# Chunked delta-rule attention with a gated MLP on one core: all five engines ordered by a planner while the kernel is built, state matmuls woven as 64x64 tiles

## The chip, the cores and the metric

The kernel runs on one core of a Trainium2 chip. The metric is the device time of one execution in microseconds (us). Before the change it is 653.14 us, the median of three runs (652.49 to 659.39).

The engines are TensorE (PE; PEld is its weight load), VectorE (DVE), ScalarE (ACT), GpSimd (POOL) and SyncE (SP), whose queue issues the DMAs. Each runs its own list of instructions in a fixed order and waits on semaphores.

## The reference

An attention with a state matrix per head, updated token by token (4 batches, 8 heads, 768 tokens, head size 48), feeds a gated MLP that also mixes over the sequence:

```python
k_n = k / (np.linalg.norm(k, axis=-1, keepdims=True) + 1e-06)
for t in range(S):
    kt, vt, bt = (k_n[:, :, t], v[:, :, t], beta[:, :, t, None])
    y[:, :, t] = np.einsum('bhd,bhde->bhe', q[:, :, t], state)
    v_old = np.einsum('bhde,bhd->bhe', state, kt)
    state = state + bt[:, :, :, None] * np.einsum('bhd,bhe->bhde', kt, vt - v_old)
...
h = np.maximum(x @ w_in, 0.0)                       # 384 -> 1024, halves u and v
v_n = (v - mu) / np.sqrt(var + 1e-06)
v_s = np.einsum('ts,bsd->btd', w_spatial, v_n) + b_spatial[None, :, None]
return ((u * v_s) @ w_out).astype(np.float32)       # 512 -> 384
```

## The kernel before

**Steps.** A batch's 768 tokens are cut into 12 chunks of 64, so there are 48 steps of one chunk of one batch, all 8 heads (4 pairs `u` of two heads `h`). Batches 0 and 2 form one chain, 1 and 3 the other; the first 6 steps belong to the first chain alone, the last 6 to the second, between them the chains take turns (`ORDER`). Within a chain a step needs the state of the one before.

**Groups and lanes.** Four steps make a group `g`. For a group the kernel computes key norms (`group_norm`), the products of keys with keys and with queries (`products`, L360, TensorE), masks them with factors that GpSimd makes (`mask_c`, L342), and inverts unit triangular matrices. The inversion is the "lanes": the matrices go through DRAM (`ad`) into a layout with one matrix per lane, then `lanes` runs 30 pairs of a product (L550) and a subtraction (L557) on VectorE on a matrix `w` in one PSUM bank (`pw`), and the result goes through DRAM (`wd`) back into `ta`. The lanes invert 32x32 blocks; `step_e` (L595) and `step_f` (L607) complete each step's 64x64 matrix. Group 0 uses blocks of 16 (`lanes16`, L444 to L496).

**A step's state work**, each eight small fp32 matmuls: `step_a` (L652, subtracts what the state predicts from v; v was scaled by GpSimd, L638), `step_b` (L669, result scaled into `su` in two halves, L673), `step_c` (L688, new state, two halves, L692), `step_d` (L702, output, with 112 and 128 rows), `step_k` (L660, copies of the masked q-k product). Every fp32 matmul leaves two records in the trace.

**The MLP** takes 256 tokens at a time. `mlp_v` (L769), `mlp_u` (L830), `mlp_g` (L849, the mixing over the sequence, possible once a batch is complete) and `mlp_o` (L894) use 128x128 matmuls in three parts (high x high, high x low, low x high). Their after-work is in `post_v`, `post_g`, `post_o` (store L905). The weights `w_in` and `w_out` are 64-bit floats decoded on VectorE (`load_w`, L157, L203).

**Order.** The author's slots (`slot_a`, `slot_cd`, `slot_b`) write out each step; `fill` puts a budget of MLP matmuls between the slots, `lane` some lane operations. Only the preparation's VectorE work is bound by hand to the written order; elsewhere a list scheduler places instructions by priority:

```python
    with tc.manual_schedule(engines={ET.DVE}):
...
    with tile.TileContext(nc, schedule_with_timeline_sim=True) as tc:
```

PSUM is shared out as 3 banks `pa` (state), 2 `pq` (products), 2 `pm` (MLP) and 1 `pw` (lanes).

Of the kernel before, what the change touches and what calls it, by code (L numbers as in the profile page):

```python
# [19 lines left out]
G = 4  # L20
DM, DFF = 384, 1024
# [7 lines left out]
R0 = 1.5  # L29
TD = 1  # L30
TP = 4
G16 = 1
C16 = 1
W16 = 16
X1 = 14
R1 = 1.7
CAP = 3.0
NL = 4
LD = 3
XD = 3  # L40
HP = 300
NW = 3
EJ = 6
PD = 2
M3 = 99
M4 = 12
CI = 1
CQ = 0
LS = 2
LP = 0  # L50
CAP0 = 4.0
PE0 = 18
PG0 = 99
PG1 = 99
VN = 1
VL = 1
DEC = 1
M5 = 10
DQ = 2
LAG = 6  # L60
# [10 lines left out]
VB = 8  # L71
UB = 4
KQB=2
NPA=3
NPQ=2
# [3 lines left out]
def delta_rule_gated_mlp(  # L79
# [3 lines left out]
    kp_t: bass.AP,  # L83
    qb_t: bass.AP,
    qa_t: bass.AP,
    kv_nat: bass.AP,
    b_nat: bass.AP,
# [7 lines left out]
    PSUM = bass.MemoryType.PSUM  # L95
    const = ctx.enter_context(tc.tile_pool(name="const", bufs=1))
    grp = ctx.enter_context(tc.tile_pool(name="grp", bufs=2))
    live = ctx.enter_context(tc.tile_pool(name="live", bufs=3))
    work = ctx.enter_context(tc.tile_pool(name="work", bufs=2))
    moe = ctx.enter_context(tc.tile_pool(name="moe", bufs=2))  # L100
    dram = ctx.enter_context(tc.tile_pool(name="dram", bufs=2, space=bass.MemoryType.DRAM))
    pa = ctx.enter_context(tc.tile_pool(name="pa", bufs=NPA, space=PSUM))
    pq = ctx.enter_context(tc.tile_pool(name="pq", bufs=NPQ, space=PSUM))
    pm = ctx.enter_context(tc.tile_pool(name="pm", bufs=7 - NPA - NPQ, space=PSUM))
    pw = ctx.enter_context(tc.tile_pool(name="pw", bufs=1, space=PSUM))

    mpos = const.tile([128, CH], F32, name="mpos")
# [11 lines left out]

    bbc = const.tile([128, SEQ], F32, name="bbc")  # L120

    hm = const.tile([128, 1], F32, name="hm")
    nc.gpsimd.memset(hm, 1.0)
    for q in range(4):
        nc.gpsimd.memset(hm[q * 32 : q * 32 + 16], 0.0)

    mcs = [const.tile([128, NU, CH], F32, name="mc0")]
    sus = []
    for i in range(4):
        su = const.tile([128, 2 * NU * HD + 16], F32, name=f"su{i}")  # L130
        nc.gpsimd.memset(su, 0.0)
        sus.append(su)

    def su_view(t, h, u, rows, w=HD):
        o = (h * NU + u) * HD
        return t[rows, o : o + w]

    def su_all(t, h, rows):
        o = h * NU * HD
        return t[rows, o : o + NU * HD].rearrange("p (u e) -> p u e", e=HD)  # L140

    win_h = const.tile([128, NK, DFF], F32R, name="win_h")
    win_l = const.tile([128, NK, DFF], F32R, name="win_l")
    wsp_h = const.tile([128, NT, SEQ], F32R, name="wsp_h")
    wsp_l = const.tile([128, NT, SEQ], F32R, name="wsp_l")
    wout_h = const.tile([128, ND, DM], F32R, name="wout_h")
    wout_l = const.tile([128, ND, DM], F32R, name="wout_l")

    count = {"dve": 0}

    class Counted:
        def __getattr__(self, name):
            fn = getattr(nc.vector, name)

            def call(*a, **k):
                count["dve"] += 1
                return fn(*a, **k)  # L157

            return call

    nv = Counted()

    def load_w(par, hi, lo, src):
        n = src.shape[1]
        tag = ("gh", "gl", "ut", "ut")[par]
        buf = moe.tile([128, 1024], F32, name="wstage", tag=tag, bufs=UB if tag == "ut" else 1)
        st = buf[:, :n]
        if src.dtype == F32:
            nc.sync.dma_start(out=st, in_=src)
            yield LD  # L170
            nc.scalar.copy(out=hi, in_=st)
            yield 0
        else:
            raw = buf[:, 512 : 512 + 2 * n].bitcast(U32).rearrange("p (n two) -> p n two", two=2)
            nc.sync.dma_start(out=raw, in_=src.bitcast(U32).rearrange("p (n two) -> p n two", two=2))
            yield LD
            w0, w1 = raw[:, :, 0], raw[:, :, 1]
            e = buf[:, 256 : 256 + n].bitcast(U32)
            nv.tensor_scalar(
                out=e, in0=w1, scalar1=20, scalar2=0x7FF, op0=ALU.logical_shift_right, op1=ALU.bitwise_and  # L180
            )
            yield 0
            if DEC:
                nc.scalar.activation(out=st, in_=w0, func=AF.Identity, scale=2.0**-52, bias=1.0)
            else:
                nv.tensor_scalar(out=st, in0=w0, scalar1=2.0**-52, scalar2=1.0, op0=ALU.mult, op1=ALU.add)
            yield 0
            nv.tensor_scalar(out=e, in0=e, scalar1=896.0, scalar2=1150.0, op0=ALU.max, op1=ALU.min)
            yield 0
            nv.tensor_scalar(  # L190
                out=e, in0=e, scalar1=896.0, scalar2=8388608.0, op0=ALU.subtract, op1=ALU.mult
            )
            yield 0
            nv.scalar_tensor_tensor(
                out=e, in0=w1, scalar=0x80000000, in1=e, op0=ALU.bitwise_and, op1=ALU.bitwise_or
            )
            yield 0
            nv.tensor_scalar(out=w1, in0=w1, scalar1=0xFFFFF, scalar2=None, op0=ALU.bitwise_and)
            yield 0
            nv.scalar_tensor_tensor(  # L200
                out=st, in0=w1, scalar=2.0**-20, in1=st, op0=ALU.mult, op1=ALU.add
            )
            nc.gpsimd.tensor_mul(out=st, in0=st, in1=e.bitcast(F32))  # L203
            yield 1
            nc.scalar.copy(out=hi, in_=st)  # L205
            yield 0
        nc.gpsimd.tensor_sub(out=lo, in0=st, in1=hi)

# [15 lines left out]

    nxt, mark = {}, {}
    tasks = []
    flags = set()

    def spawn(gen):
        tasks.append([gen, 0])  # L230

    def pump(n=1):
        for _ in range(n):
            for t in list(tasks):
                if t[1] > 0:
                    t[1] -= 1
                    continue
                try:
                    t[1] = next(t[0])
                except StopIteration:  # L240
                    tasks.remove(t)

    def pump1():
        n = count["dve"]
        for _ in range(3 * len(tasks)):
            if not tasks or count["dve"] > n:
                break
            t = tasks.pop(0)
            if t[1] > 0:
                t[1] -= 1  # L250
            else:
                try:
                    t[1] = next(t[0])
                except StopIteration:
                    continue
            tasks.append(t)

    def weights(par):
        while jobs and (par < 2 or len(jobs) > n_late):
            job = jobs.pop(0)  # L260
            yield from load_w(par, *job[:3])
            left[job[3]] -= 1
            yield 0
        flags.add(("w", par))

    def rows_d(h):
        return slice(64, 112) if h == 0 else slice(0, 48)

    def rows_t(h):
        return slice(h * 64, h * 64 + 64)  # L270

    cn_g, ta_g, ad_g, w_g = {}, {}, {}, {}

    def group_norm(g):
        s0 = g * G
        ss = grp.tile([128, G * NU], F32, name="ss")
        bn = grp.tile([128, G, NU], F32, name="bn")
        if g < 2:
            kn = moe.tile([128, 4 * NU, HD], F32, name="kn0", tag="ut", bufs=UB)
            nc.sync.dma_start(  # L280
                out=kn.rearrange("p (s u) d -> p s (u d)", s=G),
                in_=kv_nat[s0 : s0 + G, :, 0].rearrange("s p u d -> p s (u d)"),
            )
        nc.sync.dma_start(out=bn, in_=b_nat[:, s0 : s0 + G])
        yield 0
        for p in range(2):
            if g < 2:
                kp = kn[:, 2 * p * NU : 2 * (p + 1) * NU]
            else:
                kp = grp.tile([128, 2 * NU, HD], F32, name="kn", bufs=1)  # L290
                nc.sync.dma_start(
                    out=kp.rearrange("p (s u) d -> p s (u d)", s=2),
                    in_=kv_nat[s0 + 2 * p : s0 + 2 * p + 2, :, 0].rearrange("s p u d -> p s (u d)"),
                )
                yield LD
            if g == 0 and p < DQ:
                nv.tensor_mul(out=kp, in0=kp, in1=kp)
            else:
                nc.gpsimd.tensor_mul(out=kp, in0=kp, in1=kp)
                yield 0  # L300
            nv.reduce_sum(out=ss[:, p * 2 * NU : (p + 1) * 2 * NU], in_=kp, axis=AX.X)
        nr = grp.tile([128, G * NU], F32, name="nr")
        nc.scalar.activation(out=nr, in_=ss, func=AF.Sqrt)
        yield 0
        cn = grp.tile([128, G, 2, NU], F32, name="cn", bufs=4)
        t0 = grp.tile([128, G * NU], F32, name="t0")
        t3 = t0.rearrange("p (s u) -> p s u", u=NU)
        n3 = nr.rearrange("p (s u) -> p s u", u=NU)
        nv.tensor_scalar_max(out=t0, in0=nr, scalar1=1e-30)
        yield 0  # L310
# [38 lines left out]
    def products_mm(s):  # L349
        g, sl = divmod(s, G)  # L350
        while g not in cn_g:
            pump()
# [18 lines left out]
    def products_out(s, p1):  # L371
# [6 lines left out]
        if sl == G - 1:  # L378
            bounce(g)
# [898 lines left out]
```

## Time and profile before

| what | value |
|---|---|
| median of 3 runs | 653.14 us (652.49 to 659.39) |
| profiled execution | 657.81 us, span 656.1 us |
| busy, us and share | PE 547.0 (83%), PEld 478.4 (73%), DVE 407.1 (62%), ACT 270.7 (41%), POOL 201.0 (31%) |
| mean granted TensorE clock | 0.898 |
| DMA | 74.63 MB, mean 114 GB/s, all issued by SP |

The span runs from the first to the last instruction. Busy time is the time that an engine's instructions cover; matmuls overlap, so a busy TensorE is not one at its peak. The granted clock is the share of full speed that the throttle allowed. A wait is named by the instruction that ended it.

### The profile page before, as it was taken

Reading aid. Unit: us, or ns where it says so; the run is one execution under the profiler, and the core shown is the slowest. Engines: PE = TensorE matmul, PEld = TensorE weight load, DVE = VectorE, ACT = ScalarE, POOL = GpSimd, SP = SyncE. Lnnn points to the kernel's source line nnn. Section 1 sums busy time; section 2 is a strip of 40 time slices with the busy share of each in tenths; the row PEclk is TensorE's granted clock in tenths of the full one; section 3 lists DMA queues with packets and bytes.
Section 4 is the critical chain, followed back from the end, with each engine's and each line's share of the span. In section 5 each row is a group of like instructions: output and inputs, shape, how many; then the busy total and the mean of one; then the engine's idle time right before and its main releaser. Section 6 shows DMA issues by size and latency. Waiting matters only on the chain.

```text
span 656.1 us, 19076 instructions
## 1 busy us (share of the span) xinstructions
PE 547.0 (83%) x7432; PEld 478.4 (73%) x7432; DVE 407.1 (62%) x1565; ACT 270.7 (41%) x732; POOL 201.0 (31%) x251
## 2 busy tenths in 40 slices
PE   5327657785578689799999898998998999999997
PEld 4316546664567568689888776888897789998997
DVE  3579978778878768485684868626727632223142
ACT  1124233563246256452524554624227674215421
POOL 4114544654343132224432323233213134310000
PEclk9999955787579679799999898898998999999999
DMA  8553576876654653634647465253254231101001
GB/s 241 128 132 97 149 173 170 229 170 167 180 114 119 163 117 104 119 109 113 127 131 163 113 139 130 86 117 94 78 124 89 66 66 48 52 15 41 1 25 49
DMA packets 144522, 74.63 MB, mean 114 GB/s; under 512 B 105136, under 2 KB 128432, under 8 KB 144432
## 3 DMA queue, kind: packets, MB, share of 16 engines
q1 hardware_dynamic: 144432, 73.41, 44.3%
q8 instruction: 59, 0.97, 0.6%
q14 instruction: 31, 0.25, 0.1%
HBM read 58.16 MB, written 14.02 MB: 110 GB/s over the span
## 4 chain that ended last, share of the span: by engine, by line
PE 53%; DMA 17%; DVE 14%; SPq 6%; issue 4%; ACT 4%; POOL 1%; DVEq 0%; ACTq 0%; POOLq 0%
PE pm L849 13%; PE pm L830 7%; PE pm L894 6%; PE pa L702 4%; DVE wstage L157 4%; PE pa L669 3%; PE pm L769 3%; PE pq L360 3%; PE pa L688 3%; PE pa L652 3%; DMA wstage<-in_w_out 2%; DMA wstage<-in_w_in 2%; PE pa L607 2%; PE pma L849 2%; DMA kqa<-in_qa_t 2%
## 5 line engine op out<-in xcount | busy, mean ns | idle before, releaser
L557 DVE TENSOR_TENSOR pw<-pw,prod 128x120 f32<-128x120 f32 (+4 forms) x300 | 75.8, 253 | 6.6
L849 PE MATMUL pm<-wsp_h,vl 128*128 128x256 f32 x252 | 73.1, 290 | 0.0
L849 PE MATMUL pm<-wsp_h,vh 128*128 128x256 f32 x252 | 72.4, 288 | 0.0
L849 PE MATMUL pm<-wsp_l,vh 128*128 128x256 f32 x252 | 71.5, 284 | 0.0
L360 PE MATMUL pq<-kq 128*64 128x128 f32 x640 | 57.6, 315 | 10.9 <-DVE wstage L157 4.4
L638 POOL TENSOR_TENSOR v<-v,cn 128x192 f32<-128x192 f32 x48 | 24.4, 509 | 111.9 <-DMA v<-in_kv_nat 95.6
L360 PEld LDWEIGHTS pq<-kq 128*64 128x64 f32 x640 | 42.9, 157 | 18.9 <-issue 13.4
L550 DVE TENSOR_TENSOR prod<-pw,la 128x30 f32<-128x30 f32 (+4 forms) x150 | 36.6, 244 | 24.2 <-ACT pw L529 18.6
L702 PE MATMUL pa<-kqa,su 128*64 128x64 f32 (+1 forms) x768 | 43.6, 248 | 8.4 <-DVE v L655 8.4
L673 DVE TENSOR_TENSOR su<-pa,cn 64x192 f32<-64x192 f32 x96 | 33.9, 353 | 26.6 <-PE pa L669 25.4
L652 PE MATMUL pa<-su,kqa 48*64 48x48 f32 x704 | 34.6, 238 | 18.6 <-DMA kqa<-in_qa_t 11.9
L669 PE MATMUL pa<-v,ta 64*64 64x48 f32 x768 | 41.5, 242 | 9.2 <-DVE v L655 5.5
L849 PEld LDWEIGHTS pm<-wsp_h,vl 128*128 128x128 f32 x252 | 47.7, 189 | 1.6 <-issue 0.9
L652 PEld LDWEIGHTS pa<-su,kqa 48*64 48x64 f32 x704 | 28.6, 149 | 27.7 <-issue 17.4
L849 PEld LDWEIGHTS pm<-wsp_h,vh 128*128 128x128 f32 x252 | 47.7, 189 | 1.1 <-issue 0.5
L849 PEld LDWEIGHTS pm<-wsp_l,vh 128*128 128x128 f32 x252 | 47.7, 189 | 0.4
L610 ACT COPY ta<-pa 32x128 f32<-32x128 f32 x96 | 24.4, 254 | 56.9 <-PE pa L607 56.0
L669 PEld LDWEIGHTS pa<-v,ta 64*64 64x64 f32 x768 | 33.1, 152 | 16.2 <-ACT win_h L205 5.9
L702 PEld LDWEIGHTS pa<-kqa,su 128*64 128x64 f32 (+1 forms) x768 | 33.9, 154 | 15.0 <-DVE v L655 9.4
L342 POOL TENSOR_TENSOR mc<-mpos,cn 128x256 f32<-128x256 f32 x44 | 27.0, 614 | 52.5 <-DVE ta L157 45.3
L655 DVE TENSOR_TENSOR v<-v,pa 128x192 f32<-128x192 f32 x44 | 15.3, 349 | 41.3 <-PE pa L652 40.9
L660 ACT COPY kqa<-ta 64x256 f32<-64x256 f32 x96 | 38.3, 399 | 3.0 <-PE pa L702 2.2
(151 smaller groups left out, 1343.7 us busy)
## 6 DMA issues: line engine op xcount, KB each, us to landing
kq<-in_kp_t SPq DMA_DIRECT2D x40, 384.0 KB, 3.5
ad<-ta SPq DMA_DIRECT2D x24, 256.0 KB, 3.9
kqa<-in_qb_t SPq DMA_DIRECT2D x48, 128.0 KB, 2.8
kqa<-in_qa_t SPq DMA_DIRECT2D x48, 96.0 KB, 2.6
v<-in_kv_nat SPq DMA_DIRECT2D x48, 96.0 KB, 2.4
knat<-in_kv_nat SPq DMA_DIRECT2D x48, 96.0 KB, 2.5
out<-ob SPq DMA_DIRECT2D x24, 192.0 KB, 1.9
kn<-in_kv_nat SPq DMA_DIRECT2D x20, 192.0 KB, 3.2
```

The costliest lines, as they stand in the source:

```text
L342: nc.gpsimd.tensor_tensor(out=mcs[s % len(mcs)], in0=mpos.unsqueeze(1).broadcast_to([128, NU, CH]), in1=cn_g[s // G][:, s % G, 1].unsqueez ...
L360: nc.tensor.matmul(p1[rows_t(h), u], kq[:, h, u, :], kq[:, h : 3 : 2 - h, u, :], start=True, stop=True,)
L550: (nc.gpsimd if PG0 <= g < PG1 else nc.vector).tensor_tensor(out=pr, in0=w[:, :n, j : j + 1].broadcast_to([128, n, m]), in1=(la[:, j, j + ...
L557: nc.vector.tensor_add(out=w[:, :n, j + 1 : 32], in0=w[:, :n, j + 1 : 32], in1=pr)
L652: nc.tensor.matmul(pr[rows_t(h), u], kqa[rows_d(h), 1, u, :], su_view(su, h, u, rows_d(h)), start=True, stop=True)
L660: nc.scalar.copy(out=kqa[rows_t(h), 2 - 2 * h], in_=aqk[rows_t(h)])
L669: mark["pb"] = nc.tensor.matmul(pu[rows_t(h), u], tt[rows_t(h), u, :], r[rows_t(h), u, :], start=True, stop=True)
L673: mark["db"] = nc.vector.tensor_tensor(out=su_all(su, h, rows_t(h)), in0=pu[rows_t(h)], in1=cn[rows_t(h), 1].unsqueeze(2).broadcast_to([64 ...
L702: nc.tensor.matmul(py[rows_t(h), u], su_view(su, h, u, kr, 64), kqa[kr, 2 - 2 * h, u, :], start=True, stop=True)
L830: nc.tensor.matmul(pu[:, k], w[:, kt, d0 : d0 + 128], a[:, kt], start=(n == 0), stop=(n == 3 * NK - 1))
L849: nc.tensor.matmul(p[:, k], v[i][:, d0 : d0 + 128], w[:, si, ts], start=(n == 0), stop=(n == 3 * NT - 1))
L894: nc.tensor.matmul(po[:, :DM], a[:, d, ts], w[:, d], start=(n == 0), stop=(n == 3 * ND - 1))
```

## The change

The scheduler is replaced on all five engines by a planner, `Line`, that runs while the kernel is built. Each piece of work is a generator that yields operations with an engine, a time for which it is held, a time until the result is there, what it depends on, and a due date in steps. `Line.step` takes the engine that can begin earliest and there, among what can begin almost as early, the operation due first; that order is fixed in the program.

On TensorE, all state matmuls become tiles of 64 rows and 64 columns in two families: "diag" (rows and output on the same half) and "anti" (on opposite halves), with two PSUM banks each, in half-bank pieces. `Line.tensor` takes a block of one family and, if one of the other can begin, issues both alternately. MLP work goes in three to six matmuls at a time, with a rule on when to change between the two kinds. All state matmuls stand on one line, L362 (`mm`).

Lanes get two PSUM banks (`pws`), so two groups can be in work. `step_b`'s and `step_c`'s VectorE work becomes one operation each instead of two halves (L720, L748); `step_d` becomes sixteen 64x64 matmuls instead of eight; the q-k product is made in the step itself (`step_qk`). The masks (four operations of 64, L519), the scaling of v (four of 48, L642) and, from group 1 on, the squares of the norms go from GpSimd to ScalarE. `step_e`'s and `step_f`'s copies become one each. Keys and queries come as one 224 KB load (q, k) and one 112 KB load (k), with three buffers for v, k and q; the scale is copied to the other half by small DMAs (`cs`). MLP line numbers become L859 (v), L927 (u), L959 (g), L1021 (o); the two lane banks serve the MLP once the lanes are done.

```diff
+        first = min(found, key=lambda f: f[0])
+        e0, eng = first[0], first[1].eng
+        near = [f for f in found if f[1].eng == eng and f[0] <= e0 + self.SLACK[eng]]
+        if eng == "PE":
+            return self.tensor(e0, near)
+        t, op, j = min(near, key=lambda f: (f[1].due(), f[0]))
...
+        f = first([f for f in kinds["anti" if op.kind == "diag" else "diag"] if f[0] <= t + 0.2])
+        picked = [(op, j)]
+        if f:
+            picked.append(f[1:])
+            t = max(t, f[0])
+        lists = [o.make() for o, _ in picked]
+        for k in range(max(map(len, lists))):
+            for x in lists:
+                if k < len(x):
+                    x[k]()
...
+    halves = [x[:, o : o + 256] for x in banks for o in (0, 256)]
...
+    slots = {"anti": Slots(halves[:4]), "diag": Slots(halves[4:])}
...
+            x = yield act(at(("cn", t // G), ("kk", t - 2) if t >= 2 else None), d, CH)
+            nc.scalar.mul(out=mc[:, u], in_=mpos, mul=cns[t // G][:, t % G, 1, u : u + 1])
...
+                lambda p: [mm(p[rows_t(h), u], kq[rows_d(h), 0, u, :], cols(st, u, rows_d(h))) for u, h in UH],
...
+            lambda p: [mm(p[rows_s(h), u], tt[rows_t(h), u, :], v[rows_t(h), u, :]) for u, h in UH],
...
+        w = pws[g % 2].rearrange("p (i t) -> p i t", t=32)
...
+            t = yield act(at(("la", g), ("wo", g - 2) if g > 2 else None), d, 256)
...
-    with tc.manual_schedule(engines={ET.DVE}):
...
+    with tc.manual_schedule(engines={ET.PE, ET.DVE, ET.Activation, ET.Pool, ET.SP}):
```

What this does to the order, at two places. First TensorE, among the first steps, where no MLP work is ready. Before, whole blocks of different tile forms follow each other (a, f, b and e, then c and d):

```order
L652 MATMUL pa<-su_96,kqa 64x48 x8
L607 MATMUL pa<-ta,pi 32x32 x8
L360 MATMUL pq<-kq 64x128 x8
L669 MATMUL pa<-v,ta 64x48
L595 MATMUL pa<-tn,ta 32x32 x8
L669 MATMUL pa<-v,ta 64x48 x7
```

After (pt_211 and pt_212 are banks of the anti family, pt_213 and pt_214 of the diag one; the rows are a with the q-k product, then c and b alone, then another c with a):

```order
L362 MATMUL pt_211<-st_96,kq_160 64x48
L362 MATMUL pt_213<-kq_160 64x64
L362 MATMUL pt_214<-us_98,kn_156 64x48 x8
L362 MATMUL pt_212<-v_154,ta_171 64x48 x8
L362 MATMUL pt_214<-us_100,kn_157 64x48
L362 MATMUL pt_211<-st_95,kq_158 64x48
```

Blocks that stood one behind the other now alternate matmul by matmul where both families have one ready, and stand alone where not.

Second VectorE, in the middle of the lanes. Before, one group's product and subtraction alternate, between them a step's work, the state update in two halves (x2):

```order
L550 TENSOR_TENSOR prod_3175<-pw_2900,lb_2891 128x120
L557 TENSOR_TENSOR pw_2900<-pw_2900,prod_3175 128x10x12
L655 TENSOR_TENSOR v_3142<-v_3142,pa_3408 128x192
L550 TENSOR_TENSOR prod_3178<-pw_2900,lb_2891 128x110
L557 TENSOR_TENSOR pw_2900<-pw_2900,prod_3178 128x10x11
L550 TENSOR_TENSOR prod_3228<-pw_2900,lb_2891 128x110
L557 TENSOR_TENSOR pw_2900<-pw_2900,prod_3228 128x11x10
L550 TENSOR_TENSOR prod_3231<-pw_2900,lb_2891 128x99
L673 TENSOR_TENSOR su3_102<-pa_3479,cn_1620 64x192 x2
```

After, the lanes of two groups (pw0 and pw1) stand among each other:

```order
L591 TENSOR_TENSOR prod1_178<-pw1_218,la1_174 128x30
L591 TENSOR_TENSOR prod0_177<-pw0_217,lb0_175 128x96
L600 TENSOR_TENSOR pw1_218<-pw1_218,prod1_178 128x30
L748 TENSOR_TENSOR st1_95<-st0_94,pt3_214 112x192
L600 TENSOR_TENSOR pw0_217<-pw0_217,prod0_177 128x12x8
L591 TENSOR_TENSOR prod1_178<-pw1_218,la1_174 128x29
L591 TENSOR_TENSOR prod0_177<-pw0_217,lb0_175 128x84
L600 TENSOR_TENSOR pw1_218<-pw1_218,prod1_178 128x29
L600 TENSOR_TENSOR pw0_217<-pw0_217,prod0_177 128x12x7
```

An operation's neighbour is now more often of the other group, and the new state is one operation.

More of the change, by code (lines that the diff above doesn't have):

```diff
@@ L70, with before, __init__ @@
 ORDER = step_order()
[L71 to L75, printed above, removed]
+PLACE = {(b, c): s for s, (_, b, c) in enumerate(ORDER)}
+def before(s, n):
+    ch = ORDER[s][0]
+    own = [k for k in range(s) if ORDER[k][0] == ch]
+    return own[-n] if n <= len(own) else None
+class Op:
+    __slots__ = ("eng", "occ", "lat", "dep", "due", "kind", "make")
+    def __init__(self, eng, occ, lat, dep, due, kind=None, make=None):
+        self.eng, self.occ, self.lat, self.dep, self.due = eng, occ, lat, dep, due
+        self.kind, self.make = kind, make
@@ L164, in load_w, with mm, tiles_op, make @@
+    def mm(*a, **k):
+        return lambda: nc.tensor.matmul(*a, **dict(dict(start=True, stop=True), **k))
+    def tiles_op(kind, dep, d, build, w):
+        held = []
+        def make():
+            x = slots[kind].take()
+            held.append(x)
+            return build(psl(x[1], w))
+        return Op("PE", 0, 0, both(dep, slots[kind].ready), d, kind, make), held
+    def load_w(buf, hi, lo, src, d):
         n = src.shape[1]
-        tag = ("gh", "gl", "ut", "ut")[par]
-        buf = moe.tile([128, 1024], F32, name="wstage", tag=tag, bufs=UB if tag == "ut" else 1)
@@ L223, in delta_rule_gated_mlp @@
     n_late = len(jobs) - EJ
[L225 to L256, printed above, removed]
+    workers = [NW]
@@ L258, in weights @@
     def weights(par):
+        buf = (*stage, ubs[3])[par]
+        t = 0.0
         while jobs and (par < 2 or len(jobs) > n_late):
[L260 to L277, printed above, removed]
+            hi, lo, src, kind = jobs.pop(0)
+            t = yield from load_w(buf, hi, lo, src, due({"in": 3, "sp": 12, "out": 13}[kind]))
+            left[kind] -= 1
+            if left[kind] == 0:
+                done["w", kind] = t
@@ L884, in post_g @@
[L884 to L885 removed]
+        if half == 0:
+            done["ga", j] = t
+        op = either(on(t), d, 512)
+        e = nc.vector if op.eng == "DVE" else nc.gpsimd
+        t = yield op
+        e.tensor_sub(out=gl[:, hs], in0=gt, in1=gh[:, hs])
+        tmp_s.give(x, t)
+        done["g", j, half] = t
     def mlp_o(i):
@@ new lines, in load_beta, with load_bias, group @@
+    def load_beta():
+        done["ball"] = yield dma(now, due(-11.5))
+        nc.sync.dma_start(out=ball, in_=b_nat)
+    def load_bias():
+        done["bbc"] = yield dma(at("la16"), due(-2))
+        nc.sync.dma_start(out=bbc, in_=b_sp.unsqueeze(0).broadcast_to([128, SEQ]))
+    def group(g):
+        line.spawn(norm(g))
+        for t in range(g * G, g * G + G):
+            line.spawn(mask(t))
+            line.spawn(kk(t))
+        line.spawn(bounce(g))
+        if g:
+            line.spawn(load_la(g))
+            line.spawn(lanes(g))
+        else:
+            line.spawn(lanes16())
```

1621 lines of the change are left out of this document (769 added, 852 removed).

## The prediction

> **What bounds the kernel now.** I read the stages first, cut where steps begin: step 0 writes its first state update at 54 us, the 29th step at 376.3 us, the last at 584.2 us. Columns: length, busy time (and instructions) of each engine, granted TensorE clock, DMA share, GB/s.
>
> ```profile
> 0.00:54.00 54.00, 23.42 (x580) 21.14 (x580) 33.10 (x124) 12.32 (x39) 14.06 (x37) 1.00 0.61 154
> 54.00:376.30 322.30, 256.85 (x3676) 219.87 (x3678) 242.61 (x947) 138.17 (x386) 122.50 (x153) 0.81 0.56 143
> 376.30:584.20 207.90, 198.93 (x2690) 172.38 (x2691) 109.08 (x436) 96.05 (x257) 62.64 (x62) 0.97 0.36 86
> 584.20:656.00 71.80, 67.78 (x489) 65.05 (x489) 22.27 (x60) 24.20 (x52) 1.84 (x1) 0.99 0.09 30
> ```
>
> There are four regimes. A (54 us) is preparation. In B (322 us, 11.5 us a step) TensorE is 80% busy at a mean clock of 0.81 and VectorE 75%: neither is full, they wait for each other. In C (208 us, 20 steps) TensorE is 96% busy: it is the bound. D (72 us) is the rest of the MLP, TensorE alone.
>
> Second, what the busy TensorE does: a piece of its timeline in C, then rows of the chain that ended last (start, length, what, count; a state matmul leaves two records):
>
> ```profile
> 328.23 0.67 PE L652 MATMUL pa<-su,kqa 48*64 48x48 f32 x16
> 328.83 0.44 PE L607 MATMUL pa<-ta,pi 32*32 32x32 f32 x16
> 329.20 0.56 PE L688 MATMUL pa<-su,knat 64*48 64x48 f32 x16
> 329.69 0.39 PE L849 MATMUL pm<-wsp_l,vh 128*128 128x256 f32 x1
> 329.91 0.28 PE L849 MATMUL pm<-wsp_h,vl 128*128 128x256 f32 x1
> ```
>
> ```profile
> 607.17 1.40 PE pm L769 x6
> ...
> 613.13 1.40 PE pm L830 x12
> ...
> 635.38 4.26 PE pma L849 x36
> 639.64 2.09 PE pm L894 x12
> ```
>
> The MLP costs, at full clock, 864 x 0.118 (L849) + 432 x 0.117 (L830) + 216 x 0.233 (L769) + 288 x 0.174 (L894) = 253 us in both kernels. A state block of eight matmuls of 64 weight columns holds TensorE 0.60 us until the next block starts (328.23 to 328.83); the two tiles of such a block already run side by side. I split this into 8 x 0.058 = 0.46 us of streaming and 0.14 to 0.16 us for the change to another tile form; the first L849 behind a state block takes 0.22 instead of 0.118. Counting blocks in the order of the kernel before, C holds 107 us of MLP, 51 of state and 228 changes x 0.16 = 36, together 194 against 198.93 measured: the prices hold. B holds 80 + 91 + 284 x 0.16 = 216 us at full clock, over 0.81 267 us against 256.85.
>
> Third, VectorE, in order of time:
>
> ```profile
> 321.64 0.34 DVE L655 TENSOR_TENSOR v<-v,pa 128x192 f32<-128x192 f32 x1
> 321.90 0.26 DVE L557 TENSOR_TENSOR pw<-pw,prod 128x96 f32<-128x96 f32 x1
> ...
> 324.21 0.72 DVE L692 TENSOR_TENSOR su<-su,pa 48x192 f32<-48x192 f32 x2
> 324.85 0.27 DVE L557 TENSOR_TENSOR pw<-pw,prod 128x110 f32<-128x110 f32 x1
> 325.15 0.27 DVE L550 TENSOR_TENSOR prod<-pw,la 128x105 f32<-128x105 f32 x1
> 325.45 0.28 DVE L557 TENSOR_TENSOR pw<-pw,prod 128x105 f32<-128x105 f32 x1
> 325.76 0.28 DVE L550 TENSOR_TENSOR prod<-pw,la 128x120 f32<-128x120 f32 x1
> ```
>
> ```profile
> L673 DVE TENSOR_TENSOR su<-pa,cn 64x192 f32<-64x192 f32 x96 | 33.9, 353 | 26.6 <-PE pa L669 25.4
> ```
>
> The independent 192-element add L655 lets its successor start after 0.26 us; a 105-element lane operation whose successor needs its result holds the engine 0.30 us. So a start costs about 0.075 us + 1.02 ns an element, and 0.115 us more where the next one depends on it. The two halves of L692 hold it 0.64 us (324.21 to 324.85) and those of L673 twice 0.353; one whole 192-element operation would hold it 0.26.
>
> **The change part by part.** *Weaving.* All state matmuls become 64x64 tiles of two families (diagonal and anti-diagonal quadrants, different banks), and two blocks are issued alternately. No row shows four quadrants that share rows and columns. The nearest show four diagonal tiles:
>
> ```profile
> 42.80 0.73 PE L477 MATMUL pa<-la,ta 16*32 16x16 f32 x32 [19.34 <-DVE la L468]
> 43.94 0.41 PE L490 MATMUL pa<-ta,prod 32*16 32x16 f32 x32 [0.41 <-ACT prod L484]
> 45.59 0.64 PE L595 MATMUL pa<-tn,ta 32*32 32x32 f32 x16 [1.24 <-DVE prod L550]
> ```
>
> With the same 32 weight columns and a few us apart, four tiles (L477) put 32 records into 0.73 us and two tiles (L595) 16 into 0.64: twice the tiles, about twice the rate. So I take a woven slot (one matmul of each block) at the price of one matmul, 0.058 us; the other bound is no overlap, 0.116. In the new order the 3392 state matmuls fill 2209 slots, 1.54 a slot: 2209 x 0.058 = 128 us, 131 with the widening matmuls, against 158 before; with no overlap 197. Since the state keeps one tile form, only the borders between state and MLP remain as changes: 122 x 0.16 = 20 us against 547 x 0.16 = 88. TensorE at full clock: 253 + 131 + 20 = 404 us against 499.
>
> That four records can follow so closely rests on L490: 32 records in 0.41 us, 13 ns each with the drain counted. The Trainium skill ("TensorE: Matmul & The Clock Gate", "Wait — 56ns, not 53.3ns?") states that start-to-start never drops below about 25 ns however small the matmul, which would make 0.100 us of a slot of four records. L490's row does not agree with it; I keep 0.058, and a floor is a rival below.
>
> *VectorE.* Priced as above over both orders: 377 us before (219 in B), 347 after (162 in B). The two halves of the state update and of the new state become one operation each (48 x (0.71 - 0.26) + 44 x (0.64 - 0.26) = 38 us), and two groups' lanes stand alternately, so the operation behind depends less often on the one ahead (377 neighbours instead of 591). Before step 0 it is 42 us instead of 35.
>
> *Moved off GpSimd.* Masks, scaled v and squares go to ScalarE:
>
> ```profile
> L342 POOL TENSOR_TENSOR mc<-mpos,cn 128x256 f32<-128x256 f32 x44 | 27.0, 614 | 52.5 <-DVE ta L157 45.3 <-DVE cn L157 5.8 <-DVE pw L561 1.4
> L638 POOL TENSOR_TENSOR v<-v,cn 128x192 f32<-128x192 f32 x48 | 24.4, 509 | 111.9 <-DMA v<-in_kv_nat 95.6 <-DVE st L797 8.9 <-DVE pw L557 5.9
> L660 ACT COPY kqa<-ta 64x256 f32<-64x256 f32 x96 | 38.3, 399 | 3.0 <-PE pa L702 2.2
> L598 ACT COPY pi<-pa 32x128 f32<-32x128 f32 x96 | 24.7, 257 | 19.5 <-PE pa L595 17.7
> L795 ACT ACTIVATE st<-st 128x1 f32<-128x1 f32 x24 | 4.4, 196 | 0.9 <-DVE st L792 0.4
> ```
>
> On ScalarE 384 operations of 48 or 64 elements come, between half of L795's 0.196 (they are independent) and L598's 0.257: 38 to 99 us; L660 goes (38 us) and the two-part copies L598 and L610 are halved (25 us). Net -25 to +36 us over engine time of which B uses 138 of 322: covered, cost nothing; without cover at most 36.
>
> *DMA.* 552 issues on SP instead of 587, the largest (kp, 384 KB) replaced by 112 KB, and three buffers for v, k and q instead of two. Now one waiting store holds up all that is queued behind it on SP:
>
> ```profile
> SPq L905 <- ACT ob L903: 86.1, 15, 30.5
> ```
>
> ```profile
> bn<-in_b_nat SPq DMA_DIRECT2D x12, 8.0 KB, 3.3
> ```
>
> The first row is SP's own waiting, the second a kind of DMA issue (size, us to landing). The 24 new small copies of the scale (cs) are like bn, 3.3 us; each is due two steps before its use, so 0; uncovered 11 groups x 3.3 = 36 us. New in SP's queue is that the prefetches of q, v and k wait for buffers in a fixed order; the work behind them is a step's a, b and d. With v and the masks off GpSimd, what is late next is the lanes' way through DRAM and back (ad, la, wd, ta).
>
> **The sum.** A: 54 + 7 us more VectorE, of which I count half: 58. B in the new order: MLP 53, state 72, 62 changes 10, TensorE 135 us instead of 216; VectorE 162 instead of 219. Scaled by TensorE, 322 x 135/216 = 201; by VectorE, 322 x 162/219 = 238; I take 215, nearer TensorE's, because dependence between neighbours, which makes VectorE wait for itself, is what the order reduces. C: 107 + 50 + 54 x 0.16 = 166 us; before needed 207.9 for 194, so x 1.07 = 178. D: behind the last state matmul stand 93 us of MLP (before, behind the last update, 66 in 71.8): 93 + 6 = 99. Span 58 + 215 + 178 + 99 = 550 against 656.1. The profiled execution took 657.81, 4.7 above the median 653.14 and 1.7 above its span, so against the median I subtract 3: **547 us**. Its own range, from 201 and 238 in B and 166 to 190 in C, is 510 to 585.
>
> **Rivals.** *Fuller queues.* VectorE packed to 85% in B (190 us), C 172, A 55, D 97: 511. For it: nothing in C or D waits for VectorE. Against: 0.68 is what B reached before.
>
> *VectorE sets B.* The lanes still wait on their own results: B 238, 570 in all. For it: the new order shows each group's lanes ending just ahead of the group's first step.
>
> *The weave does not do what it says.* Quadrants that share rows or columns run one after the other: B 322 x 174/216 = 259, C (107 + 77 + 9) x 1.07 = 207: 620. For it: no row shows such sharing; against: L477.
>
> *A floor per record.* L607's block takes 0.37 us for 16 records (328.83 to 329.20), 23 ns each with the change counted; if no record can be shorter, the 1184 woven slots of four cost 0.093 us. That adds 41 us at full clock, split as the state is: B +34, C +17, 598 in all. L490 stands against it. The Trainium skill's floor ("TensorE: Matmul & The Clock Gate", "Wait — 56ns, not 53.3ns?") is of this size.
>
> *Slower: the clock.* Woven tiles leave TensorE idle more often within each few us, and the granted clock stays at half. B and C hold 301 us of TensorE work; A and D take 157. The time reaches 653 when 301/c = 499, so from a mean clock of 0.60 down it is slower; at 0.55 it is 701. For it: B now runs at 0.81, with half-clock stretches. Against: TensorE's load in B falls only from 216/322 = 67% to 135/215 = 63%. The Trainium skill ("TensorE: Matmul & The Clock Gate", "Part 1: The HAM clock gate") says that the clock falls to half after an idle window of about 3.4 us; the stretches' 0.81 and 0.97 agree that a denser stretch gets more of it.
>
> **How the numbers follow.** The forecast has 0.49, fuller queues 0.10, VectorE 0.14, no overlap 0.11, the floor 0.03, the clock 0.13. The range 500 to 640 leaves out most of the clock case and the ends. About 1% is what a measurement of this kernel can tell from no change. Faster: 0.49 + 0.10 + 0.14 + 0.03 + 0.09 of no overlap = 0.85; within 1%: 0.03 (the rest of no overlap, and a mild clock case); slower: 0.12.
>
> **What would show it.** Right: 32 records of a woven pair start within about 0.5 us at full clock; the 29th step's update (L720) comes near 273 us and the last near 450; TensorE is then dense for about 99 us at clock 1; the mean clock before the 29th step lies near 0.8; GpSimd is under 110 us. Wrong: woven pairs that take 0.9 us (no overlap), a clock below 0.6, or VectorE over 85% busy before the 29th step. A long wait on SP that holds a step's loads would make the order itself the fault.

## The result, and the profile after

The changed kernel takes 617.71 us (median of 3 runs, 614.33 to 619.30) against 653.14: ratio 0.942, 95% interval 0.931 to 0.953. It is faster, inside the range of 500 to 640, but by 35 us where 106 were forecast. Medians are over all runs, while ratios and intervals leave out runs that fell in a slower state of the chip, so the two can differ a little. The profiled execution took 617.71 us, span 616.0. Columns are as in the prediction. Cut at the same events (first, 29th and last state update, now L720):

```profile
0.00:64.60 64.60, 21.73 (x624) 19.89 (x624) 45.99 (x191) 35.91 (x128) 15.65 (x42) 0.68 0.67 164
64.60:308.90 244.30, 188.66 (x4229) 168.36 (x4230) 173.89 (x788) 138.50 (x447) 56.28 (x53) 0.76 0.57 135
308.90:514.20 205.30, 185.95 (x3276) 168.43 (x3276) 112.06 (x449) 103.60 (x304) 23.56 (x18) 0.92 0.35 83
514.20:616.00 101.80, 95.96 (x712) 93.07 (x712) 34.23 (x76) 27.94 (x59) 0.00 (x0) 1.00 0.07 25
```

| stage | before | forecast | measured | miss |
|---|---|---|---|---|
| A | 54.0 | 58 | 64.6 | 7 |
| B | 322.3 | 215 | 244.3 | 29 |
| C | 207.9 | 178 | 205.3 | 27 |
| D | 71.8 | 99 | 101.8 | 3 |

The miss sits in B and C, where state steps run. The planner's own dates for the three updates are 52.5, 223.3 and 400.6 us: the run falls 12 us behind them in A, 74 in B and 28 in C, in small pieces. In B no engine is full: TensorE 77% busy, VectorE 71%, ScalarE 57%. The work moved to ScalarE is dearer than I had priced it, and ScalarE is now more of the chain that ended last (11%, before 4%). Two groups of the page, then one v on ScalarE's timeline (start, length, what, count), then the chain by engine before, and by engine and line after:

```profile
L519 ACT ACTIVATE mc<-mpos,cn 128x64 f32<-128x64 f32 x192 | 51.0, 338 | 9.0 <-DVE cn L507 5.1
L642 ACT ACTIVATE v<-v,cn 128x48 f32<-128x48 f32 x192 | 48.8, 327 | 11.7 <-DMA v<-in_kv_nat 11.5
```

```profile
70.27 1.01 ACT L642 ACTIVATE v<-v,cn 128x48 f32<-128x48 f32 x4
71.19 0.35 ACT L673 ACTIVATE pi<-pt,hl 128x128 f32<-128x128 f32 x1
```

```profile
PE 53%; DMA 17%; DVE 14%; SPq 6%; issue 4%; ACT 4%; POOL 1%; DVEq 0%; ACTq 0%; POOLq 0%
```

```profile
PE 52%; DVE 15%; DMA 12%; ACT 11%; issue 4%; SPq 4%; POOL 0%; DVEq 0%; ACTq 0%
PE pt L362 22%; PE pm L959 8%; PE pw L959 6%; PE pm L927 5%; PE pm L859 3%; DVE prod L591 3%; DVE pw L600 3%; PE pw L1021 3%; DMA kq<-in_kq_t 3%; PE pm L1021 3%; DMA knn<-in_kv_nat 2%; ACT v L642 2%; ACT mc L519 2%; DMA wstage<-in_w_in 2%; PE pw L859 1%
```

Four multiplies of 48 elements hold ScalarE from 70.27 to 71.19, 0.23 us each; the planner counts 0.087 us. Over the whole trace, the median from one multiply's start to the next one's is 0.226 us for 48 elements and 0.239 for 64.

The weave works as priced. Where two blocks alternate at full clock, four records start in 0.058 us (k with tn below); where one stands alone, two records take that (4 in 0.12 us from 256.68 to 256.80):

```profile
255.81 0.23 PE L362 MATMUL pt<-k 48*64 48x64 f32 x2
255.84 0.23 PE L362 MATMUL pt<-tn,ta 64*64 64x32 f32 x2
255.87 0.23 PE L362 MATMUL pt<-k 48*64 48x64 f32 x2
...
256.68 0.28 PE L362 MATMUL pt<-aq,us 64*64 64x64 f32 x4
256.80 0.28 PE L362 MATMUL pt<-kq,st 48*64 48x64 f32 x4
256.92 0.28 PE L362 MATMUL pt<-aq,us 64*64 64x64 f32 x4
```

The same stretch shows what the prediction does not have. VectorE's L543 reads the first half of a bank; its block of k put its last records there at 253.97 (first fence below). It starts 3.3 us later, and 0.27 us after the last record of d (256.98, in the last row above), which the program put into the second half of the same bank. Meanwhile VectorE is idle for 1.29 us:

```profile
253.97 0.32 PE L362 MATMUL pt<-k 48*64 48x64 f32 x2
```

```profile
255.67 0.22 DVE L591 TENSOR_TENSOR prod<-pw,lb 128x65 f32<-128x65 f32 x1
255.81 0.15 DVE L882 TENSOR_SCALAR sm<-sm 128x1 f32<-128x1 f32 x1
257.25 0.42 DVE L543 TENSOR_TENSOR ta<-pt,mc 128x256 f32<-128x256 f32 x1 [1.29 <-PE pt L362]
257.59 0.22 DVE L600 TENSOR_TENSOR pw<-pw,prod 128x65 f32<-128x65 f32 x1
```

The wait in the compiled program names the last of those d matmuls, the 64th behind the block's own last one. It holds over 60 such waits of VectorE and ScalarE for a later matmul of the other half (the expectation of h1 below counts 62, by 1382 matmuls in sum), and at least as many waits of TensorE for a reader of the other half; the planner, which dates each block by itself, knows of none. The Trainium skill ("PSUM — Partial Sum Buffer", "PSUM bank collisions raise a hardware error") says that two engines must never touch one bank on the same 32 partitions at once, whichever columns. The trace shows the wait, and no run here tries to go without it.

SP's own waiting, foreseen as "one waiting store", is large. Most of the store's (L1033) lies in C and D; the loads of q and k (L635) and of v (L639) wait 88 us in all for matmuls that still read their buffers. What that costs a step stays open, as no run here has more buffers (total, times, longest):

```profile
SPq L1033 <- ACT ob L1030: 126.6, 23, 27.0
SPq L635 <- PE pt L362: 47.1, 32, 10.6
SPq L639 <- PE pt L362: 41.4, 27, 10.1
```

### The profile page after: what moved, and what is told of

Its sections match the earlier page's. It is cut to its first block, busy times and chain, and to the rows that moved or that the text cites. A ratio compares the mean times of both kernels' runs of the same rounds, so it can differ in the third digit from the quotient of the medians.

```text
span 616.0 us, 21605 instructions
## 1 busy us (share of the span) xinstructions
PE 492.3 (80%) x8840; PEld 449.7 (73%) x8840; DVE 366.2 (59%) x1500; ACT 306.0 (50%) x936; POOL 95.5 (16%) x113
## 4 chain that ended last, share of the span: by engine, by line
PE 52%; DVE 15%; DMA 12%; ACT 11%; issue 4%; SPq 4%; POOL 0%; DVEq 0%; ACTq 0%
PE pt L362 22%; PE pm L959 8%; PE pw L959 6%; PE pm L927 5%; PE pm L859 3%; DVE prod L591 3%; DVE pw L600 3%; PE pw L1021 3%; DMA kq<-in_kq_t 3%; PE pm L1021 3%; DMA knn<-in_kv_nat 2%; ACT v L642 2%; ACT mc L519 2%; DMA wstage<-in_w_in 2%; PE pw L859 1%
## 5 line engine op out<-in xcount | busy, mean ns | idle before, releaser
L600 DVE TENSOR_TENSOR pw<-pw,prod 128x96 f32<-128x96 f32 (+11 forms) x330 | 81.4, 251 | 4.8
L362 PE MATMUL pt<-kq,st 48*64 48x64 f32 x768 | 63.4, 255 | 0.6 <-DVE us L720 0.6
L362 PE MATMUL pt<-aq,us 64*64 64x64 f32 x768 | 61.3, 251 | 0.8 <-DVE us L720 0.4
L959 PE MATMUL pm<-wsp_h,vh 128*128 128x256 f32 x192 | 56.2, 293 | 0.0
L519 ACT ACTIVATE mc<-mpos,cn 128x64 f32<-128x64 f32 x192 | 51.0, 338 | 9.0 <-DVE cn L507 5.1
L959 PE MATMUL pm<-wsp_h,vl 128*128 128x256 f32 x192 | 54.7, 285 | 0.0
L959 PE MATMUL pm<-wsp_l,vh 128*128 128x256 f32 x192 | 54.7, 285 | 0.0
L642 ACT ACTIVATE v<-v,cn 128x48 f32<-128x48 f32 x192 | 48.8, 327 | 11.7 <-DMA v<-in_kv_nat 11.5
L362 PEld LDWEIGHTS pt<-aq,us 64*64 64x64 f32 x768 | 51.3, 165 | 1.2 <-DVE us L720 0.5
L362 PEld LDWEIGHTS pt<-kq,st 48*64 48x64 f32 x768 | 51.3, 164 | 1.1 <-DVE us L720 0.8
L362 PE MATMUL pt<-tn,ta 64*64 64x32 f32 x768 | 37.9, 247 | 17.7 <-DVE tn L659 12.2
L362 PE MATMUL pt<-k 48*64 48x64 f32 x640 | 32.1, 257 | 21.4 <-DVE wstage L405 10.5
L362 PEld LDWEIGHTS pt<-tn,ta 64*64 64x64 f32 x768 | 33.7, 165 | 20.0 <-DVE tn L659 19.3
L362 PE MATMUL pt<-v,ta 64*64 64x48 f32 x768 | 42.3, 257 | 6.4 <-DVE v L704 2.8
L591 DVE TENSOR_TENSOR prod<-pw,la 128x30 f32<-128x30 f32 (+5 forms) x165 | 40.1, 245 | 11.6 <-ACT pw L579 4.8
L362 PE MATMUL pt<-ta,pi 64*64 64x32 f32 x768 | 39.6, 249 | 9.1 <-ACT pi L673 8.7
L362 PE MATMUL pt<-kq 48*64 48x64 f32 x768 | 41.7, 262 | 5.8 <-DMA kq<-in_kq_t 5.8
L362 PEld LDWEIGHTS pt<-v,ta 64*64 64x64 f32 x768 | 35.5, 169 | 13.2 <-DVE v L704 3.7
L362 PE MATMUL pt<-us,kn 64*64 64x48 f32 x704 | 36.6, 252 | 10.5 <-DVE us L720 6.3
L362 PE MATMUL pt<-st,kq 48*64 48x48 f32 x704 | 35.8, 248 | 11.2 <-DMA kq<-in_kq_t 4.8
## 6 DMA issues: line engine op xcount, KB each, us to landing
out<-ob SPq DMA_DIRECT2D x24, 192.0 KB, 1.9
knn<-in_kv_nat SPq DMA_DIRECT2D x20, 192.0 KB, 3.3
```

What stands on the lines that cost most here:

```text
L362: return lambda: nc.tensor.matmul(*a, **dict(dict(start=True, stop=True), **k))
L519: nc.scalar.mul(out=mc[:, u], in_=mpos, mul=cns[t // G][:, t % G, 1, u : u + 1])
L591: nc.vector.tensor_tensor(out=pr, in0=w[:, :n, j : j + 1].broadcast_to([128, n, m]), in1=(la[:, j, j + 1 : 32] if j < 16 else lb[:, j - 16 ...
L600: nc.vector.tensor_add(out=w[:, :n, j + 1 : 32], in0=w[:, :n, j + 1 : 32], in1=pr)
L642: nc.scalar.mul(out=vts[s % 3][:, u], in_=vts[s % 3][:, u], mul=cns[s // G][:, s % G, 0, u : u + 1])
L959: nc.tensor.matmul(pg[:, k], v[:, d0 : d0 + 128], w[:, si, ts], start=(n == 0), stop=(n == 3 * NT - 1))
```

## The experiments

The theories: T1, the order is built on a ScalarE that the planner holds too fast; T2, ScalarE's load costs wherever it stands; T3, half clock and latency between short blocks; later, the shared bank. Each kernel was timed in 3 rounds against the kernel before. Ratios are to before; the changed kernel has 0.942. Two control orders of it (k1, k2, below) have 0.942 and 0.938, and with e1 and g5, which are other orders of the same instructions too, its five orders span 609 to 619 us. So single differences under some 10 us are not told apart.

**The weave alone.** Never pick a second block (e4_noweave):

```diff
-        if f:
-            picked.append(f[1:])
-            t = max(t, f[0])
```

> The changed kernel with each state block issued alone, never two alternately; same tiles, same engines. If weaving is worth on the chip what its slots are worth (2209 slots become 3392, each 0.058 us: 69 us of TensorE), 655 to 685 us. T3 (weaving shortens blocks, but the next block waits for the same VectorE or ScalarE result, so little of it comes through): 615 to 635.

657.46 us, 1.005 [1.000, 1.009]. Weaving is worth 40 us, more than orders of one kernel differ by (up to 19 us below), and the whole gain of the change: without it, all other parts together (planner, ScalarE's new work, bigger blocks) come to nothing. Of the 69 us of slots that it saves, 40 come through.

**ScalarE's multiplies.** Priced truly in the planner (e1), moved to GpSimd (e2) or VectorE (e3) as one broadcast multiply each. `act2` holds ScalarE 0.172 us + 1.05 ns an element; the second part is e2, and e3 has `dve` and `nc.vector` there; the masks likewise:

```diff
-            x = yield act(both(on(t), at(("cn", s // G))), due(s - 1.5), HD)
+            x = yield act2(both(on(t), at(("cn", s // G))), due(s - 1.5), HD)
...
+        x = yield pool(both(on(t), at(("cn", s // G))), due(s - 1.5), 192)
+        nc.gpsimd.tensor_tensor(
```

> Same instructions as the changed kernel (617.7 us); only the order differs, because the planner now holds ScalarE 0.24 us for a scaled 64-element multiply (it held 0.103), 0.22 for 48 elements (0.087), 0.26 for the masked copy and 0.71 for two 512-element activations with a per-partition bias. T1 (the order is built on a ScalarE that is too fast, so work that is late stands ahead of work that is ready): 580 to 600 us; the 29th step's update comes before 290 us. T2 (ScalarE's 100 us of small multiplies cost what they cost, wherever they stand): 610 to 625. T3 (the lost time is half clock on TensorE and latency between short blocks): 610 to 625 as well.

> Masks and scaled v go back to GpSimd, one broadcast multiply each (88 operations, about 0.61 and 0.51 us), everything else as in the changed kernel; the 384 multiplies leave ScalarE (its busy time falls by about 100 us). T1 and T2 (ScalarE's load is the fault): 570 to 595 us. T3 (half clock and latency between blocks): 610 to 625. If GpSimd's long operations become the wait: above 625.

> Masks and scaled v as one VectorE multiply each: 40 x 0.34 + 48 x 0.28 = 27 us more on VectorE, 100 us less on ScalarE. T1 and T2: 575 to 600 us. T3: 610 to 625. If VectorE sets the middle stage (its planned share there is already the highest): over 620.

e1 608.62 us (0.933 [0.926, 0.940]), e2 600.05 (0.915 [0.907, 0.924]), e3 624.30 (0.957 [0.949, 0.964]). The plan's price matters little: e1 lies near the controls, its B is even 248.7 us. The load itself costs: off ScalarE and on GpSimd, the time falls by 18 us (by 9 to 19 against the five orders), less than expected. On VectorE it is no gain: e3 keeps VectorE busy 401 us where e2 has 371, and takes 24 us longer than e2, so VectorE's load counts too.

**Half clock.** The granted clock was 0.76 in B. 544 idle matmuls where TensorE stood idle, order unchanged (f1), and the same on e2 (f2):

```diff
+            for _ in range(n):
+                nc.tensor.matmul(x, win_h[:, 0, 0:128], win_h[:, 0, 0:256], start=True, stop=True)
```

> The changed kernel in its own order, with 544 idle 128x128 matmuls of 256 columns (0.118 us each, 64 us in all) added at 69 places where TensorE stood idle for over 0.35 us between 58 and 514 us of its trace; each gap is filled to four fifths, and their results are read by nobody. Theory clock (the middle stages run at half clock because TensorE rests too often; half clock costs about 31 us in the middle stage and 16 in the last third): the granted clock goes to about 1, 570 to 595 us. Theory waits (the path goes through VectorE, ScalarE and DMA results, and TensorE's speed hides behind them): 612 to 625 us at a higher clock. If the idle places move, so that the added matmuls delay real ones: over 625.

> The variant with masks and scaled v on GpSimd (600.1 us), with 475 idle matmuls (56 us) at the 66 places where its own trace showed TensorE idle for over 0.35 us. Theory clock: 555 to 580 us. Theory waits: 595 to 606.

f1: 611.53 us (0.932 [0.921, 0.942]); f2: 605.16 (0.924 [0.915, 0.933]) where e2 had 600.05. B and C of f1:

```profile
68.90:305.20 236.30, 217.18 (x4626) 194.51 (x4627) 173.07 (x788) 137.58 (x447) 56.13 (x53) 0.96 0.60 141
305.20:507.90 202.70, 191.83 (x3413) 175.72 (x3413) 111.47 (x449) 103.56 (x303) 23.58 (x18) 0.99 0.35 83
```

B's clock rises from 0.76 to 0.96, and B is 8 us shorter, C 3, while A became 4 longer. The idle matmuls write to a free half of a state bank, so they can add waits of the kind shown above, and this run alone would not settle it. But kernels without idle matmuls say the same where their executions differ in the mean granted clock: k1 took 614.76 us at 0.849 and 614.71 at 0.927, g4 609.25 at 0.885 and 609.52 at 0.947. TensorE's speed was hidden behind waits: my theory that half clock ate the gain fell.

**Two other steps of the prediction.** Lanes one group at a time (g4: the dependence `("wo", g - 2)` becomes `("wo", g - 1)`), and landing times 0.8 us longer in the planner (g5: `lat + 0.8`):

> The changed kernel, but a group's lanes start only when the group before has copied its result out, so VectorE never alternates between two groups. If the alternation is worth what the prediction counted (about 250 fewer dependent neighbours x 0.115 us = 25 us of VectorE in the middle stage): 630 to 645 us. If VectorE's idle 70 us in that stage absorb it: 612 to 624.

> Same instructions as the changed kernel; the planner believes that every transfer lands 0.8 us later than it did (2.6 becomes 3.4 us and so on; the trace has 2.6 to 4.1). If transfers that come later than planned cause the stalls: 595 to 608 us. If not: 612 to 630.

g4 609.75 us (0.936 [0.927, 0.946]), g5 619.32 (0.947 [0.939, 0.955]). Neither is told apart from the control orders: here the alternation of two groups bought nothing.

**One block per bank** (h1; h3 with e2's multiplies and the true price of ScalarE's other biased operations; h5 with e1's prices):

```diff
-    halves = [x[:, o : o + 256] for x in banks for o in (0, 256)]
+    halves = [x[:, 0:256] for x in banks]
...
-    slots = {"anti": Slots(halves[:4]), "diag": Slots(halves[4:])}
+    slots = {"anti": Slots(halves[:2]), "diag": Slots(halves[2:])}
```

> The changed kernel with one state block per PSUM bank (the first half of each of the four banks, two blocks of a family in flight) instead of two halves of a bank, each for another block. Theory bank: dependences are kept per bank, so a reader of one half waits for the matmuls written to the other half that stand ahead of it in the order, and a block waits for the reader of the other half; the planner does not know this, so its order slips by a step's latency again and again. In the changed kernel 62 waits on TensorE are later than they need to be by 1382 matmuls in sum, 62 waits of TensorE on the others likewise; here none. By this theory 575 to 600 us, though half the slots are left (the planner itself dates the end 7 us later). Theory many small causes (half clock, ScalarE's price, transfers): 612 to 630, since fewer slots only take freedom away.

> One block per bank, and masks and scaled v on GpSimd (which alone gave 600.1 us), with ScalarE's other biased activations held at their true length in the planner. Theory bank: 555 to 585 us. Theory many small causes: 598 to 612.

> One block per bank, and ScalarE's scaled multiplies held at their true length in the planner (which alone gave 608.6 us). Theory bank: 565 to 595 us. Theory many small causes: 606 to 622.

h1 603.97 us (0.920 [0.914, 0.926]), h3 585.67 (0.895 [0.887, 0.903]), h5 605.36 (0.923 [0.917, 0.928]). Half the slots, and faster by 14 us, just short of what I expected; together with e2's change by 32, 1 us short of the range. But h5 missed: with e1's prices, one block per bank is worth 3 us (605.4 after 608.6) where the bank theory asked for 14 or more. The stages of the profiled executions show where the gain goes:

| run | A | B | C | D | B and C |
|---|---|---|---|---|---|
| changed kernel | 64.6 | 244.3 | 205.3 | 101.8 | 449.6 |
| h1, one block per bank | 74.8 | 224.6 | 202.2 | 101.8 | 426.8 |
| e1 | 62.6 | 248.7 | 191.5 | 102.2 | 440.2 |
| h5, one block per bank | 71.3 | 226.3 | 204.4 | 102.2 | 430.7 |
| e2 | 63.7 | 237.4 | 196.4 | 101.8 | 433.8 |
| h3, one block per bank | 67.6 | 220.2 | 192.5 | 102.2 | 412.7 |

In all three pairs B and C together fall, by 23, 10 and 21 us, and A, with half the slots, takes 10, 9 and 4 back. B and C are taken together because the orders share the MLP out between them differently. A and B of h1 word for word:

```profile
0.00:74.80 74.80, 28.66 (x688) 25.83 (x688) 53.26 (x219) 39.13 (x140) 18.64 (x46) 1.00 0.60 149
74.80:299.40 224.60, 179.32 (x4141) 156.83 (x4142) 165.23 (x759) 133.43 (x439) 51.60 (x48) 0.87 0.62 146
```

VectorE's idle time ahead of the two readers of whole halves, in the changed kernel and in h1 (busy, mean ns | idle before):

```profile
L764 DVE TENSOR_TENSOR aq<-pt,mpos 128x256 f32<-128x256 f32 x48 | 20.0, 418 | 11.6 <-PE pt L362 10.9 <-ACT pi L673 0.3 <-ACT ta L685 0.3
L543 DVE TENSOR_TENSOR ta<-pt,mc 128x256 f32<-128x256 f32 x48 | 19.9, 420 | 21.3 <-PE pt L362 14.3 <-issue 2.3 <-ACT xs L793 2.1
```

```profile
L764 DVE TENSOR_TENSOR aq<-pt,mpos 128x256 f32<-128x256 f32 x48 | 19.9, 415 | 3.7 <-PE pt L362 3.3
L543 DVE TENSOR_TENSOR ta<-pt,mc 128x256 f32<-128x256 f32 x48 | 19.9, 417 | 9.4 <-PE pt L362 7.7 <-ACT mc L519 1.5
```

**What is left**, tried on h3: idle matmuls (i1), lanes one after the other (i2), true landing times for k, q and the norm's keys (i3).

> The variant with one block per bank and GpSimd masks (585.7 us), with 294 idle matmuls (35 us) at 50 places where TensorE stood idle in its trace. Its middle stage still runs 90 us at half clock. If that half clock is what is left of the miss: 560 to 575 us. If TensorE's speed hides behind waits there too: 580 to 592.

> The same variant (585.7 us) with the groups' lanes one after the other. The planner dates its end 9 us later. If the alternation pays once the false waits are gone: 592 to 600 us. If it is worth nothing, as in the changed kernel (609.8 against 617.7): 578 to 590.

> The same variant (585.7 us) with the planner's landing times for k and q (2.6 to 4.2 us) and the keys of the norm (3.0 to 4.6 us) set to what its trace shows on the path. Transfers are 17% of its chain that ended last. If late landings hold the order up: 568 to 580 us. If not, or if the planner only gives the waits another place: 582 to 600.

i1 590.67 us (0.898 [0.888, 0.907]): B's clock rises from 0.79 to 0.91, and the time does not fall, so the clock is not what is left. i2 603.25 (0.922 [0.917, 0.928]): 10 to 20 us above three orders of this variant (583 to 594: h3 and two controls below). i3 601.63 (0.924 [0.917, 0.931]): the same instructions as h3, and 16 us longer. Its order leaves less MLP for the end (D is 63.7 us, C 243.5). So late landings are not shown to be what is left, and since an order alone can cost this much, what lanes in turn cost (i2) is not told apart from a worse order.

**Controls.** Is this cause or luck of the order? Another PAIR in the changed kernel (k1 0.95, k2 1.2) and in h3 (k3, k4):

> A control: the changed kernel (617.7 us) with one number of the planner's taste altered (PAIR 1.0 to 0.95, which decides when a pair of state blocks goes ahead of the MLP). The same instructions in an equally good order: the planner dates the end 4 us earlier. If the 14 and 17 us of the experiments stand for their causes: 611 to 621. If any other order moves the time by as much: below 608 or above 628.

> The same control with PAIR 1.2; the planner dates the end 1 us earlier. Causes real: 612 to 624 us. Order by chance worth as much: below 608 or above 628.

> The control on the variant with one block per bank and GpSimd masks (585.7 us), PAIR 0.95. Causes real: 578 to 592 us, still below every order of the changed kernel. Chance: above 598.

> The same with PAIR 1.2. Causes real: 580 to 594 us. Chance: above 598.

k1 615.01 us (0.942 [0.936, 0.947]), k2 612.36 (0.938 [0.930, 0.945]); k3 582.59 (0.888 [0.880, 0.895]), k4 593.56 (0.909 [0.900, 0.917]). The two sets of three orders do not touch: 612 to 618 against 583 to 594, 28 us between the means, 615.0 and 587.3. With the other runs that only reorder the same instructions they still do not: e1 and g5 make the first 609 to 619, i3 makes the second 583 to 602. So both causes together are shown (h3, k3 and k4 also hold some of ScalarE's other operations at their true length in the planner, which no run takes out). Each alone is shown less firmly: e2 and h1 lie 12 and 8 us below the best control, but 9 and 5 below e1, and h5 3 below it. k3 is the fastest kernel here, 5.7% faster than the changed one by the medians, and the stages of its profiled execution (575.8 us) are:

```profile
0.00:69.70 69.70, 28.48 (x688) 25.40 (x688) 57.10 (x216) 21.59 (x64) 30.35 (x65) 1.00 0.66 160
69.70:279.90 210.20, 172.02 (x4129) 151.72 (x4130) 167.82 (x756) 86.70 (x229) 80.38 (x100) 0.92 0.65 154
279.90:471.90 192.00, 179.77 (x3312) 163.61 (x3312) 113.88 (x455) 81.21 (x202) 38.07 (x44) 0.97 0.37 89
471.90:574.10 102.20, 96.19 (x715) 93.14 (x712) 34.21 (x76) 28.24 (x59) 0.00 (x0) 1.00 0.07 25
```

## Why the prediction was right or wrong

- **Right: the weave's price.** A slot of two matmuls takes 0.058 us at full clock; neither "no overlap" nor "a floor per record" came true, and four records in 0.058 us are 15 ns each. D was right (101.8 for 99), GpSimd too (95.5, under 110).
- **Wrong: "covered, cost nothing".** The 384 ScalarE operations were bounded by 38 and 99 us; they take nearly the upper end (192 x 0.239 + 192 x 0.226 = 89 us of starts). The squares that moved along (L483, 11 us) stand in no term of the sum. ScalarE's busy time rose by 35 us, inside the -25 to +36 of the prediction, so the step erred in the cover: B's ScalarE load, 138 of 322 us before, is 138.5 of 244 after, and v (L642) and masks (L519) stand on the chain that ended last. This is worth 9 to 19 us (e2). The Trainium skill ("ScalarE: Activation LUTs", "What ACT_TABLE_LOAD costs") gives such an operation 186 ns + 93 ns per pointer operand + 0.833 ns an element, less 93 ns of overlap with its neighbour. An estimate from these figures is 226 and 239 ns between starts; the trace agrees (0.226 and 0.239 us).
- **Wrong: B "scaled by TensorE".** The engines' own work was counted nearly right: TensorE is busy 188.7 us at a mean clock of 0.76, an estimated 143 us at full clock where I had 135, and VectorE 174 where I had 162. What failed is the rule that B's length goes with TensorE's work. It supposes that TensorE sets the pace there, and f1, with TensorE at 0.96 of full speed, gains 8 us in B. ScalarE's load was on the path, and two blocks in one bank, which the sum takes as free of each other, wait for each other's readers and writers. The second costs 3 to 14 us in all (h5, h1, h3), of which B gives 20 in h1 (244.3 to 224.6) and A takes back 10. With both causes gone B is 210 to 220 us (k3, h3, k4), around the 215 that I took.
- **The rival "VectorE sets B"** came near in the number (238 for 244.3). VectorE is busy 71% of B, less than the 75% before, so it does not set B alone; that its load counts is what e3 shows. These runs do not settle more.
- **Wrong: C's 166 us of TensorE, times 1.07.** TensorE is busy 186 of C's 205.3 us, 20 more than the sum, and idle 19 where the factor allowed 12. Its MLP matmuls were as many as counted (106.7 us at the prediction's prices), so what was too small lies in the state work, the changes of form and the clock (0.92 here). In k3 the idle time is the 12 allowed (179.8 busy of 192.0); that TensorE's work is 14 over the sum stays. How it splits is not known, and k4 has 198.4.
- **A's sum was short.** VectorE had 46.0 us there where I counted 42, and ScalarE went from 12.3 to 35.9. ScalarE is not the reason: in e2 it has 17.9 us there, and A is still 63.7. What is stays open.
- **The clock rival** needed a mean clock of 0.60 or less, and the kernel had 0.842 (0.76 in B, before 0.81). The clock did fall, but the fall cost little: f1 and i1 raise the clock and gain little or nothing.
- **Two groups' lanes:** worth nothing in the changed kernel (g4). Without the bank's waits they may be worth 10 to 20 us (i2), but i3 shows an order without that change as slow.
- **Open:** some 36 us from k3's 582.6 to 547. Its profiled execution, 7 us faster than its median, is 24 over the forecast span of 550: C 14, A 12, D 3, B 5 under. Neither clock (i1) nor landing times (i3) was shown to be the cause.

## What to carry to other kernels

A saving on the busiest engine comes through only as far as no other link of the step grows: price what moved to the "idle" engine at its measured start-to-start time, and ask whether the step waits for it. When PSUM is cut into halves of a bank, count the bank as the unit of waiting; here two banks of a family with one block each beat two with two, by 3 to 14 us, though that halves the slots. Before a difference of 2% between two orders is called a cause, run the same instructions in another order or two: here that alone moved the time by up to 11 us in one kernel and 19 in another.

## What was not expected of the hardware

A multiply of 48 or 64 elements by a per-partition scale starts every 226 or 239 ns on ScalarE; on VectorE one operation of 256 elements holds the engine 0.34 us for all four (L543, from 257.25 to 257.59). And TensorE at a granted clock of 0.96 instead of 0.76 through all of B shortened that stage by 8 us of 244: in this stage, where no engine was full, the clock of one hardly showed.
